# Attention and gated experts on one core: gate weights loaded behind the first exponential, keys turned behind the first scores, loads and stores priced by their own rate

## The chip, the cores and the metric

One core of one Trainium2 chip. The metric is device time of one execution in microseconds.

## What is computed

Eight batches; q, k, v have 8 heads, 576 positions and 64 columns, p has 32 rows a head. Attention runs twice, then each token goes through the expert that its gate picks, or that of the token before it where its local gate is at least 0.5.

```python
p_packed = sm_attn(p, k, v)                # softmax(p k^T / 8) v
out = sm_attn(q, p_packed, p_packed)       # x: 8 x 576 x 512
logits = einsum('bsd,de->bse', x, w_gate)
e = argmax(logits[b, s]) if s == 0 or sigmoid(x @ w_local)[b, s] < 0.5 else prev_e
h = maximum(x[b, s] @ w1[e], 0.0)          # 512 -> 1024
out[b, s] = softmax(logits[b, s])[e] * (h @ w2[e])
```

## The kernel before

The kernel takes one batch after the other. It takes the expert chosen for the batch's first token for the whole batch and mends tokens for which this doesn't hold. Per batch, for two halves of four heads each (Q0 and Q1): the keys are turned (a transpose) into `qn`, scores of p against them go to PSUM (`scores`, L477), an exponential follows (L506), its weights `a` are turned (L515, L520) into `a1T`, the packed values come from L540, are scaled into `zz` (L553) and turned into `ppT` (L561). Against `ppT` the gate of a batch's first token is computed (L701 to L733), which gives the expert `e`; its weights `w1t` and `w2raw` are then fetched by SP. The second attention (L591 to L645) gives `a2t`, cast into `a2h` with a remainder `a2l` (L651, L654). The first layer never forms x: W1 is multiplied with `ppT` (L889 in batch 0, L918 in the others) into `wph` and its remainder `wpl`, and L958 multiplies those with `a2h` and `a2l`; L969 and L973 make `h`; the second layer (L986, L991, L995) multiplies it with `w2s`, a rounded `w2raw` and its remainder (L944, L946). L1009 to L1021 scale by the gate into `o`, which is stored.

In batches 0 and 1 keys and queries are turned on TensorE (`turn_tokens`, L422 and L430, tile `kw` for the long part, `qt` for the rest) and p in `turn_packs` (L458); in the others VectorE turns them (L444, L575). `heat` is a bf16 tile on which dummy matmuls (L217) are run where PE would be idle in the head. `load_small` fetches three small inputs on ScalarE's DMA queue; `wgl` holds `w_gate` in 64 x 8 x 8, in rows of 8 elements, and gets a ninth column from `small` by VectorE (`turn_small`, L296).

All instructions are in an order that is decided when the program is built. Each piece of work is a generator that yields what it needs (`need`: tiles, free slots, a condition, and by whom a tile is consumed). `weave` starts, at each step, a generator that the `Clock` believes ready; `Clock.note` adds each instruction to the modelled time of its engine. DMAs all went to one modelled queue, at `clock.rate` bytes per ns, which keeps the value that was last set. So a price changes which instruction comes first on an engine, and nothing else.

Of the kernel before, what the change touches and what calls it, by code (L numbers as in the profile page):

```python
# [16 lines left out]
DRAM = bass.MemoryType.DRAM  # L17
# [5 lines left out]
NQ = H // HQ  # L23
# [34 lines left out]
class Clock:  # L58
# [69 lines left out]
    def note(self, inst):  # L128
        outs = [x.bass_ap for x in inst.outs if hasattr(x, "bass_ap")]
        ins = [x.bass_ap for x in inst.ins if hasattr(x, "bass_ap")]  # L130
# [6 lines left out]
        dma = inst.opcode == "DMACopy"  # L137
        if dma:
            kind, took = "DMA", min(x.free_size() * x.partition_size() for x in outs + ins if x.space != DRAM) * 4 / self.rate
        else:  # L140
            kind, took = self.price(inst, outs, ins)
        start = max(self.engine(kind), self.engine("SP") if dma else 0.0)
        for x in ins + ([] if dma else outs):
            at, by = self.written.get(self.key(x), (0.0, kind))
# [18 lines left out]
def packed_attn_moe_kernel(  # L163
# [12 lines left out]
    nc = tc.nc  # L176
# [103 lines left out]
    def load_small():  # L280

        clock.rate = 100.0
        nc.scalar.dma_start(out=small[0:2 * H], in_=q[0:2, :, 0, :].rearrange("b h d -> (b h) d"))
        nc.scalar.dma_start(out=small[2 * H:3 * H], in_=w_local.rearrange("(h d) e -> h (d e)", d=D))
        with nc.allow_non_contiguous_dma(reason="rows of 8 elements"):
            nc.scalar.dma_start(out=wgl[:, :, 0:E], in_=w_gate.rearrange("(h d) e -> d h e", d=D))
# [84 lines left out]
    def loads(st):  # L371
# [12 lines left out]
        for name, Q in order:  # L384
# [3 lines left out]
            if name == "q" and isinstance(b, int) and b == 2:  # L388
                yield need(when=lambda: len(sts[1].get("w1", ())) == 2)
            yield need(slot="p_in" if name == "p" else "qn" if blocks else "kv" if name == "v" else ("w2s", "o"))  # L390
            if name == "p":
# [17 lines left out]
    def turn_tokens(st, name):  # L409
# [5 lines left out]
        for Q in range(NQ):  # L415
            yield need(when=lambda: (name, Q) in st and (early or st["second"] or st["valued"] == NQ and (Q == 0 or st["ppT"][Q] is not None)))
            x, rest = st[name, Q]
            for n, hs in enumerate((slice(0, 2), slice(2, 4))):
                yield need(x[:, hs], banks=1, by=("Activation",))
                tp = bank()  # L420
                for c in range(4):
                    nc.tensor.transpose(out=tp[:, 128 * c:128 * c + 128], in_=x[:, hs][:, c // 2, 128 * (c % 2):128 * (c % 2) + 128], identity=ident)  # L422
                yield need(tp, by=("Activation",))
                (nc.vector.tensor_copy if early and Q == 0 and n else nc.scalar.copy)(
                    out=xT[:, Q, hs, 0:256].rearrange("a h (p c) -> a h c p", c=2), in_=tp.rearrange("a (h c p) -> a h c p", h=2, c=2),
                )
                give(tp)
# [24 lines left out]
    def turn_packs(st):  # L452

        yield need(when=lambda: "px" in st)
        yield need(st["px"], slot="pT", banks=1, by=("Activation",))
# [165 lines left out]
    def soften(st, Q, part, m0, m1, sT):  # L621
# [27 lines left out]
        give(sT)  # L649
        yield need(a2t)  # L650
        nc.scalar.copy(out=a2h, in_=a2t)  # L651
# [348 lines left out]
    def store(b, st, i, mask=None):  # L1000
# [23 lines left out]
        if mask is not None:  # L1024
# [4 lines left out]
            )  # L1029
        queue = nc.scalar if isinstance(b, int) and b == B - 1 and i == 3 else nc.sync  # L1030
        queue.dma_start(out=dst, in_=o[:rows])

# [89 lines left out]
    def weave(main):  # L1122
# [3 lines left out]
        while main in threads or any(x.batch < 0 for x in threads):  # L1126
# [7 lines left out]
            while started < B and started <= max(at_batch[0], 0) + AHEAD:  # L1134
# [4 lines left out]
                    slots(st), pack_quarters(st) if early else pack_weights(st, both), splits(st),  # L1139
                    *((turn_small(),) if early else ()), *((early_choice(st),) if started < 2 else ()),  # L1140
                    *((turn_packs(st), turn_tokens(st, "k")) if started < 2 else (turn_keys(st, Q) for Q in both)),
# [148 lines left out]
```

## Time and profile before

| | us |
|---|---|
| median of three runs | 431.81 (431.33 to 433.35) |
| profiled execution | 430.42 |
| its span | 428.6 |
| outside the span | 1.82 |
| PE busy | 410.8 (96%) |
| VectorE busy | 292.4 (68%) |
| ScalarE busy | 180.8 (42%) |
| GpSimd busy | 46.8 (11%) |
| DMA moved | 73.10 MB |

The span is what the hardware profiler recorded from the first to the last instruction. Busy times of different engines overlap. PE is matmul, DVE VectorE, ACT ScalarE, POOL GpSimd, SPq and ACTq the engines' DMA issues. A row of the timeline is a run of like instructions (x16), with its start, how long it took, and in brackets how long the engine had been idle before and what ended that.

### The profile page before, as it was taken

Reading aid. Unit: us, or ns where it says so; the run is one execution under the profiler, and the core shown is the slowest. Engines: PE = TensorE matmul, PEld = TensorE weight load, DVE = VectorE, ACT = ScalarE, POOL = GpSimd, SP = SyncE. Lnnn points to the kernel's source line nnn. Section 1 sums busy time; section 2 is a strip of 40 time slices with the busy share of each in tenths; the row PEclk is TensorE's granted clock in tenths of the full one; section 3 lists DMA queues with packets and bytes.
Section 4 is the critical chain, followed back from the end, with each engine's and each line's share of the span. In section 5 each row is a group of like instructions: output and inputs, shape, how many; then the busy total and the mean of one; then the engine's idle time right before and its main releaser. Section 6 shows DMA issues by size and latency. Waiting matters only on the chain.

```text
span 428.6 us, 9926 instructions
## 1 busy us (share of the span) xinstructions
PE 410.8 (96%) x3784; PEld 320.0 (75%) x3785; DVE 292.4 (68%) x853; ACT 180.8 (42%) x420; POOL 46.8 (11%) x65
## 2 busy tenths in 40 slices
PE   6999999999998999999999999999999999999994
PEld 3646677878885788776888688777887678878883
DVE  1478558887779797749975778749966688547321
ACT  2455453365333633345333544154434533344211
POOL 2001520253130002000110001100030001100000
PEclk9999999999999999999999999999999999999998
DMA  8849739999998599906998299945999430563011
GB/s 222 239 136 326 219 71 160 319 192 211 130 120 297 154 201 151 335 11 211 167 162 308 79 240 133 237 164 158 181 130 269 151 111 0 163 216 125 0 63 57
DMA packets 161671, 73.10 MB, mean 171 GB/s; under 512 B 126288, under 2 KB 141648, under 8 KB 161616
## 3 DMA queue, kind: packets, MB, share of 16 engines
q1 hardware_dynamic: 160624, 72.04, 73.8%
q8 instruction: 32, 0.52, 0.5%
q10 hardware_dynamic: 992, 0.35, 0.3%
q14 instruction: 23, 0.19, 0.1%
HBM read 62.94 MB, written 9.44 MB: 169 GB/s over the span
## 4 chain that ended last, share of the span: by engine, by line
PE 76%; DVE 8%; SPq 5%; DMA 5%; issue 2%; ACT 2%; POOLq 0%; POOL 0%; DVEq 0%; ACTq 0%
PE bank L986 37%; PE bank L958 21%; PE bank L991 4%; PE bank L995 3%; PE bank L540 2%; PE bank L918 2%; DVE wpl L932 2%; PE bank L591 2%; PE bank L515 2%; PE bank L477 2%; DMA kv<-in_q_dram 1%; DMA qn<-in_q_dram 1%; SPq L324 1%; DVE qn L575 1%; DVE h L973 1%
## 5 line engine op out<-in xcount | busy, mean ns | idle before, releaser
L986 PE MATMUL bank<-w2s,h 128*128 128x512 f32 x768 | 207.4, 400 | 4.6 <-DVE w2s L946 3.1
L986 PEld LDWEIGHTS bank<-w2s,h 128*128 128x128 f32 x768 | 135.4, 188 | 35.6 <-issue 5.2
L969 ACT ACTIVATE h<-bank 128x256 fp32r<-128x256 f32 (+1 forms) x128 | 52.9, 413 | 116.8 <-PE bank L958 111.9
L973 DVE SCALAR_TENSOR_TENSOR h<-bank,h 128x256 fp32r<-128x256 f32 x192 | 61.5, 348 | 58.6 <-ACT h L969 58.3
L958 PEld LDWEIGHTS bank<-a2h,wph 128*128 128x128 f32 x256 | 47.0, 188 | 17.4 <-ACT wph L929 2.3
L958 PE MATMUL bank<-a2h,wph 128*128 128x320 f32 (+1 forms) x256 | 56.9, 302 | 0.3
L958 PE MATMUL bank<-a2h,wpl 128*128 128x320 f32 (+1 forms) x256 | 55.9, 298 | 0.1
L958 PE MATMUL bank<-a2l,wph 128*128 128x320 f32 (+1 forms) x256 | 54.6, 294 | 0.0
L654 POOL TENSOR_TENSOR a2l<-a2t,a2h 128x576 fp32r<-128x576 f32 (+2 forms) x17 | 23.4, 1377 | 275.0 <-ACT a2h L651 275.0
L958 PEld LDWEIGHTS bank<-a2h,wpl 128*128 128x128 f32 x256 | 41.0, 188 | 1.0 <-DVE wpl L932 1.0
L958 PEld LDWEIGHTS bank<-a2l,wph 128*128 128x128 f32 x256 | 41.0, 188 | 0.0
L944 ACT CAST w2s<-w2raw 128x512 fp32r<-128x512 f32 x64 | 37.4, 625 | 2.6 <-DMA w2raw<-in_moe_w_dram 2.4
L946 DVE TENSOR_TENSOR w2s<-w2raw,w2s 128x512 fp32r<-128x512 f32 x50 | 32.4, 683 | 0.8 <-ACT w2s L944 0.7
L991 PE MATMUL bank<-w2s,h 128*128 128x512 f32 x64 | 26.0, 406 | 0.0
L995 PE MATMUL bank<-w2s,h 128*64 128x512 f32 x64 | 25.2, 394 | 0.0
L932 DVE TENSOR_TENSOR wpl<-bank,wph 128x512 fp32r<-128x512 f32 x28 | 18.3, 683 | 6.8 <-ACT wph L929 6.8
L946 POOL TENSOR_TENSOR w2s<-w2raw,w2s 128x512 fp32r<-128x512 f32 x14 | 17.9, 1300 | 27.4 <-ACT w2s L944 22.6
L929 ACT CAST wph<-bank 128x512 fp32r<-128x512 f32 x28 | 14.8, 599 | 11.5 <-PE bank L918 11.5
L485 DVE TENSOR_SCALAR_CACHE_REDUCE a<-bank 128x288 f32<-128x288 f32 x32 | 13.3, 454 | 8.7 <-PE bank L477 8.2
L611 DVE STREAM_TRANSPOSE sT<-bank 128x288 f32<-128x288 f32 (+2 forms) x36 | 13.2, 419 | 8.5 <-ACT gate L609 7.9
L651 ACT CAST a2h<-a2t 128x576 fp32r<-128x576 f32 (+2 forms) x18 | 11.1, 625 | 13.2 <-DVE a2t L645 10.3
L575 DVE STREAM_TRANSPOSE qn<-qn 128x1152 f32<-128x1152 f32 x12 | 16.5, 1373 | 0.1
(148 smaller groups left out, 451.4 us busy)
## 6 DMA issues: line engine op xcount, KB each, us to landing
w2raw<-in_moe_w_dram SPq DMA_DIRECT2D x64, 256.0 KB, 7.3
w1t<-in_moe_w_dram SPq DMA_DIRECT2D x14, 1024.0 KB, 5.8
kv<-in_v_dram SPq DMA_DIRECT2D x16, 512.0 KB, 6.3
out_dram<-o SPq DMA_DIRECT2D x31, 256.0 KB, 2.7
qn<-in_k_dram SPq DMA_DIRECT2D x24, 288.0 KB, 7.1
qn<-in_q_dram SPq DMA_DIRECT2D x24, 288.0 KB, 7.5
w1t<-in_moe_w_dram SPq DMA_DIRECT2D x4, 512.0 KB, 6.3
kw<-in_k_dram SPq DMA_DIRECT2D x3, 512.0 KB, 6.8
```

The costliest lines, as they stand in the source:

```text
L575: nc.vector.transpose(out=qT, in_=qT)
L654: eng.tensor_tensor(out=a2l, in0=a2t, in1=a2h.bitcast(F32), op=ALU.subtract)
L929: nc.scalar.copy(out=hi[fh][:, Q], in_=ts[fh, Q])
L932: nc.vector.tensor_tensor(out=lo[fh][:, Q], in0=ts[fh, Q], in1=hi[fh][:, Q].bitcast(F32), op=ALU.subtract)
L944: nc.scalar.copy(out=w[:, 0], in_=raw)
L946: (nc.gpsimd if st["second"] or st["early"] and c > 1 else nc.vector).tensor_tensor(out=w[:, 1], in0=raw, in1=w[:, 0].bitcast(F32), op=ALU ...
L958: nc.tensor.matmul(out=t[:, :GROUP * (m1 - m0)], lhsT=st["wp"][c // 4][wi][:, Q, fs], rhs=a2[ai][Q][:, GROUP * m0:GROUP * m1], start=(n == ...
L969: nc.scalar.activation(out=h[:, :w], in_=t[:, :w], func=AF.Relu)
L973: nc.vector.scalar_tensor_tensor(out=h[:, dst:dst + z - a], in0=t[:, a:z], scalar=0.0, in1=h[:, a:z].bitcast(F32), op0=ALU.max, op1=ALU.su ...
L986: nc.tensor.matmul(out=acc, lhsT=hs[hi], rhs=w[:, wi], start=(c == 0 and n == 0), stop=(c == NC - 1 and n == 2),)
L991: nc.tensor.matmul(out=acc, lhsT=h[:, 256:WIDE + TAIL], rhs=w[:, 0], start=(c == 0), stop=False, skip_group_check=True,)
L995: nc.tensor.matmul(out=acc[0:TAIL], lhsT=h[:, 256:WIDE], rhs=w[:, 1], start=False, stop=(c == NC - 1), skip_group_check=True,)
```

## The change

The load of `wgl` moves from `load_small` into a generator of its own that starts once the exponential of Q0 is issued. The second half of batch 0's keys is turned only after the first half has been scored, and half of its copy goes to VectorE. The packs of batch 1 are turned only after batch 0's expert is chosen. DMAs of ScalarE's queue get a modelled queue of their own, stores a rate of 300 bytes per ns, and the cast of `a2t` says that only ScalarE consumes it. The slot asked for by a q load of the second batch is another one.

```diff
--- before.py
+++ after.py
@@ -136,10 +136,11 @@
             return
         dma = inst.opcode == "DMACopy"
         if dma:
-            kind, took = "DMA", min(x.free_size() * x.partition_size() for x in outs + ins if x.space != DRAM) * 4 / self.rate
+            aside = "Activation" in str(inst.engine)
+            kind, took = "DMA2" if aside else "DMA", min(x.free_size() * x.partition_size() for x in outs + ins if x.space != DRAM) * 4 / self.rate
         else:
             kind, took = self.price(inst, outs, ins)
-        start = max(self.engine(kind), self.engine("SP") if dma else 0.0)
+        start = max(self.engine(kind), self.engine("Activation" if aside else "SP") if dma else 0.0)
         for x in ins + ([] if dma else outs):
             at, by = self.written.get(self.key(x), (0.0, kind))
             start = max(start, at + (LAT if by != kind else 0.0 if kind == "PE" else SAME))
@@ -282,6 +283,11 @@
         clock.rate = 100.0
         nc.scalar.dma_start(out=small[0:2 * H], in_=q[0:2, :, 0, :].rearrange("b h d -> (b h) d"))
         nc.scalar.dma_start(out=small[2 * H:3 * H], in_=w_local.rearrange("(h d) e -> h (d e)", d=D))
+
+    def load_gates():
+
+        yield need(when=lambda: sts[0]["weighed"] > 0)
+        clock.rate = 100.0
         with nc.allow_non_contiguous_dma(reason="rows of 8 elements"):
             nc.scalar.dma_start(out=wgl[:, :, 0:E], in_=w_gate.rearrange("(h d) e -> d h e", d=D))
 
@@ -387,7 +393,7 @@
                 yield need(when=lambda: all("w2" in sts[x] and len(sts[x]["w2"]) == NC for x in (b - 2, b - 1) if "ereg" in sts[x]))
             if name == "q" and isinstance(b, int) and b == 2:
                 yield need(when=lambda: len(sts[1].get("w1", ())) == 2)
-            yield need(slot="p_in" if name == "p" else "qn" if blocks else "kv" if name == "v" else ("w2s", "o"))
+            yield need(slot="p_in" if name == "p" else "qn" if blocks else "kv" if name == "v" else ("kv" if name == "q" and st["second"] else "w2s", "o"))
             if name == "p":
                 if st["pairs"]:
                     st["px"] = load_packs(b, (nc.sync, nc.sync))
@@ -413,7 +419,7 @@
         xT = st[name] = tile_([128, NQ, HQ, HALF], F32, "qn")
         clock.halves[xT.tensor.name] = H * HALF
         for Q in range(NQ):
-            yield need(when=lambda: (name, Q) in st and (early or st["second"] or st["valued"] == NQ and (Q == 0 or st["ppT"][Q] is not None)))
+            yield need(when=lambda: (name, Q) in st and (early and (Q == 0 or st["scored"] > 0) or st["second"] or st["valued"] == NQ and (Q == 0 or st["ppT"][Q] is not None)))
             x, rest = st[name, Q]
             for n, hs in enumerate((slice(0, 2), slice(2, 4))):
                 yield need(x[:, hs], banks=1, by=("Activation",))
@@ -421,7 +427,7 @@
                 for c in range(4):
                     nc.tensor.transpose(out=tp[:, 128 * c:128 * c + 128], in_=x[:, hs][:, c // 2, 128 * (c % 2):128 * (c % 2) + 128], identity=ident)
                 yield need(tp, by=("Activation",))
-                (nc.vector.tensor_copy if early and Q == 0 and n else nc.scalar.copy)(
+                (nc.vector.tensor_copy if early and n else nc.scalar.copy)(
                     out=xT[:, Q, hs, 0:256].rearrange("a h (p c) -> a h c p", c=2), in_=tp.rearrange("a (h c p) -> a h c p", h=2, c=2),
                 )
                 give(tp)
@@ -451,7 +457,7 @@
 
     def turn_packs(st):
 
-        yield need(when=lambda: "px" in st)
+        yield need(when=lambda: "px" in st and (st["early"] or "ereg" in sts[0]))
         yield need(st["px"], slot="pT", banks=1, by=("Activation",))
         tp = bank()
         for g in range(2):
@@ -647,7 +653,7 @@
                 in_=sT[:, r].rearrange("a m n -> a (m n)"),
             )
         give(sT)
-        yield need(a2t)
+        yield need(a2t, by=("Activation",))
         nc.scalar.copy(out=a2h, in_=a2t)
         yield need(a2h)
         eng = nc.vector if part == 0 and Q == 1 else nc.gpsimd
@@ -1028,6 +1034,7 @@
                 out=o[:rows], mask=mask[:rows, i:i + 1].broadcast_to([rows, DM]), data=new[:rows],
             )
         queue = nc.scalar if isinstance(b, int) and b == B - 1 and i == 3 else nc.sync
+        clock.rate = 300.0
         queue.dma_start(out=dst, in_=o[:rows])
 
     def chunks(todo, aside, mask=None):
@@ -1137,7 +1144,7 @@
                 apart = tuple((Q,) for Q in both) if early else (both,)
                 threads.extend(Thread(g, started) for g in (
                     slots(st), pack_quarters(st) if early else pack_weights(st, both), splits(st),
-                    *((turn_small(),) if early else ()), *((early_choice(st),) if started < 2 else ()),
+                    *((load_gates(), turn_small()) if early else ()), *((early_choice(st),) if started < 2 else ()),
                     *((turn_packs(st), turn_tokens(st, "k")) if started < 2 else (turn_keys(st, Q) for Q in both)),
                     *(scores(st, Qs) for Qs in (apart if started != 1 else ((0,), (1,)))), *(keys(st, Qs) for Qs in apart),
                     *((gate_weights(st),) if started < 2 else ()), gates(st),
```

How the order moves, at three places. On PE in the head, before (`kw`, `qt` are keys, `heat` dummies, L477 the scores of Q0 and then Q1):

```order
22 L217 LDWEIGHTS heat
23 L217 MATMUL bank_68<-heat 128x512
24 L422 MATMUL bank_188<-ident,kw 128x128 x4
25 L477 MATMUL bank_193<-qn,pT 32x288 x4
26 L477 MATMUL bank_194<-qn,pT 32x288 x4
27 L422 MATMUL bank_208<-ident,kw 128x128 x4
28 L430 MATMUL bank_214<-ident,qt 128x128
29 L217 LDWEIGHTS heat
...
37 L477 MATMUL bank_225<-qn,pT 32x288 x4
38 L477 MATMUL bank_226<-qn,pT 32x288 x4
```

and now (L428 was L422, L483 was L477, L436 was L430):

```order
24 L218 LDWEIGHTS heat
25 L218 MATMUL bank_68<-heat 128x512
26 L483 MATMUL bank_188<-qn,pT 32x288 x4
27 L483 MATMUL bank_189<-qn,pT 32x288 x4
28 L428 MATMUL bank_202<-ident,kw 128x128 x4
29 L428 MATMUL bank_208<-ident,kw 128x128 x4
30 L436 MATMUL bank_214<-ident,qt 128x128
31 L218 LDWEIGHTS heat
32 L218 MATMUL bank_68<-heat 128x512
...
41 L483 MATMUL bank_227<-qn,pT 32x288 x4
42 L483 MATMUL bank_228<-qn,pT 32x288 x4
```

The scores of Q0 now stand ahead of all three turning steps of Q1, with one dummy more before them.

On VectorE where batch 1's first layer is prepared, before:

```order
164 L973 SCALAR_TENSOR_TENSOR h<-bank_1276,h 128x256
165 L642 TENSOR_TENSOR sT<-sT,sm 128x576
166 L645 STREAM_TRANSPOSE a2t<-sT 128x288 x2
167 L973 SCALAR_TENSOR_TENSOR h<-bank_1298,h 128x256
168 L444 STREAM_TRANSPOSE qn<-qn 128x4x288
169 L760 STREAM_TRANSPOSE lt<-bank_1326 128x160
170 L973 SCALAR_TENSOR_TENSOR h<-bank_1318,h 128x256
171 L407 STREAM_TRANSPOSE p_in<-p_in 128x256
172 L932 TENSOR_TENSOR wpl<-bank_1356,wph 128x512
173 L932 TENSOR_TENSOR wpl<-bank_1357,wph 128x512
```

and now (L651 was L645, L450 was L444, L938 was L932):

```order
164 L979 SCALAR_TENSOR_TENSOR h<-bank_1275,h 128x256
165 L646 RECIPROCAL sm<-sm 128x18
166 L648 TENSOR_TENSOR sT<-sT,sm 128x576
167 L450 STREAM_TRANSPOSE qn<-qn 128x4x288
168 L979 SCALAR_TENSOR_TENSOR h<-bank_1295,h 128x256
169 L938 TENSOR_TENSOR wpl<-bank_1317,wph 128x512
170 L938 TENSOR_TENSOR wpl<-bank_1318,wph 128x512
171 L979 SCALAR_TENSOR_TENSOR h<-bank_1342,h 128x256
172 L651 STREAM_TRANSPOSE a2t<-sT 128x288 x2
173 L938 TENSOR_TENSOR wpl<-bank_1319,wph 128x512
174 L938 TENSOR_TENSOR wpl<-bank_1320,wph 128x512
```

The second pair of `a2t` now stands behind a turn of `qn`, two `h` and two `wpl`.

On VectorE in batch 3, where `w2s` is prepared, before:

```order
382 L932 TENSOR_TENSOR wpl<-bank_2809,wph 128x512
383 L932 TENSOR_TENSOR wpl<-bank_2810,wph 128x512
384 L575 STREAM_TRANSPOSE qn<-qn 128x4x288
385 L973 SCALAR_TENSOR_TENSOR h<-bank_2853,h 128x256
386 L973 SCALAR_TENSOR_TENSOR h<-bank_2853,h 128x64
387 L932 TENSOR_TENSOR wpl<-bank_2811,wph 128x512
388 L1021 TENSOR_SCALAR o<-bank_2537,pe 128x512
389 L932 TENSOR_TENSOR wpl<-bank_2812,wph 128x512
390 L946 TENSOR_TENSOR w2s<-w2raw,w2s 128x512
391 L575 STREAM_TRANSPOSE qn<-qn 128x4x288
```

and now (L952 was L946, L581 was L575):

```order
381 L938 TENSOR_TENSOR wpl<-bank_2752,wph 128x512
382 L938 TENSOR_TENSOR wpl<-bank_2753,wph 128x512
383 L559 TENSOR_SCALAR zz<-bank_2792,rs 128x128 x2
384 L979 SCALAR_TENSOR_TENSOR h<-bank_2779,h 128x256
385 L938 TENSOR_TENSOR wpl<-bank_2754,wph 128x512
386 L938 TENSOR_TENSOR wpl<-bank_2755,wph 128x512
387 L952 TENSOR_TENSOR w2s<-w2raw,w2s 128x512 x2
388 L581 STREAM_TRANSPOSE qn<-qn 128x4x288
```

Two `w2s` now stand ahead of the turn of `qn` that was before all of them.

## Rows read from the trace of the kernel before

**Rows 1.** Windows: length, busy by engine, PEclk, DMA share, GB/s

```profile
0.00:26.00 26.00, 21.37 (x261) 12.81 (x263) 9.74 (x45) 10.41 (x27) 2.71 (x18) 0.93 0.70 194
...
33.20:52.00 18.80, 18.48 (x159) 13.06 (x158) 13.57 (x46) 9.53 (x24) 5.65 (x5) 1.00 0.97 289
...
52.00:104.00 52.00, 51.87 (x590) 40.30 (x592) 38.69 (x130) 25.48 (x63) 12.97 (x15) 1.00 0.85 189
```

**Rows 2.** PE's waits, 52 us to the end: total, times, longest

```profile
PE bank L986 <- DVE w2s L946: 3.1, 3, 1.1
```

**Rows 3.** Timeline, 9 to 14.3: start, us, engine, line

```profile
9.16 0.99 PE L422 MATMUL bank<-ident,kw 128*128 128x128 f32 x4 [2.12 <-DMA kw<-in_k_dram]
...
10.09 1.21 PE L477 MATMUL bank<-qn,pT 64*32 64x288 f32 x16
...
12.35 1.23 PE L217 MATMUL bank<-heat 128*128 128x512 bf16 x4
...
13.03 0.79 ACT L506 ACTIVATE a<-a,nb 128x576 f32<-128x576 f32 x1
...
13.51 0.71 PE L477 MATMUL bank<-qn,pT 64*32 64x288 f32 x16
```

**Rows 4.** Windows of the head, columns as in rows 1

```profile
10.00:11.00 1.00, 1.00 (x17) 0.23 (x16) 0.00 (x0) 0.63 (x1) 0.00 (x0) 0.50 1.14 283
...
13.00:14.00 1.00, 1.00 (x19) 0.26 (x17) 0.00 (x0) 0.92 (x3) 0.00 (x0) 1.00 0.94 301
...
22.00:25.00 3.00, 2.12 (x29) 1.12 (x24) 1.78 (x10) 1.82 (x5) 0.00 (x0) 1.00 0.05 12
```

**Rows 5.** Timeline, 18 to 24.5, VectorE and PE

```profile
18.16 0.15 DVE L296 COPY wgl<-bank 64x8 f32<-64x8 f32 x1
...
19.23 0.35 DVE L553 TENSOR_SCALAR zz<-bank,rs 128x128 f32<-128x128 f32 x1 [0.92 <-PE bank L540]
...
22.30 0.66 PE L422 MATMUL bank<-ident,kw 128*128 128x128 f32 x4
...
22.80 0.25 DVE L720 STREAM_TRANSPOSE et<-es 128x64 f32<-128x64 f32 x1
...
23.84 0.41 PE L458 MATMUL bank<-ident,p_in 128*128 128x128 f32 x2 [0.88 <-DMA p_in<-in_p_dram]
...
24.17 0.31 PE L723 MATMUL bank<-gate,et 128*32 128x32 f32 x4
```

**Rows 6.** DMA queues, 4.5 to 8: packets, MB, share of 16 engines

```profile
q1 hardware_dynamic: 996, 0.91, 87.1%
...
q10 hardware_dynamic: 527, 0.02, 8.3%
```

**Rows 7.** Timeline of ScalarE's DMA issues

```profile
2.45 0.70 ACTq L286 DMA_DIRECT2D wgl<-in_moe_w_gate_dram  x1
```

**Rows 8.** DMA queues, 8 to 12, columns as in rows 6

```profile
q1 hardware_dynamic: 1533, 1.12, 112.7%
```

**Rows 9.** DMA issues, 0 to 40: KB each, median us to landing

```profile
kv<-in_v_dram SPq DMA_DIRECT2D x4, 512.0 KB, 7.8
...
small<-in_q_dram ACTq DMA_DIRECT2D x1, 4.0 KB, 3.0
```

**Rows 10.** Timeline, 81 to 88.5, around batch 1's first layer

```profile
81.02 0.84 DVE L645 STREAM_TRANSPOSE a2t<-sT 128x288 f32<-128x288 f32 x2
...
81.90 0.68 ACT L651 CAST a2h<-a2t 128x576 fp32r<-128x576 f32 x1
...
82.65 1.42 POOL L654 TENSOR_TENSOR a2l<-a2t,a2h 128x576 fp32r<-128x576 f32 x1 [0.36 <-ACT a2h L651]
...
86.83 1.29 DVE L932 TENSOR_TENSOR wpl<-bank,wph 128x512 fp32r<-128x512 f32 x2 [1.48 <-ACT wph L929]
...
88.05 0.45 PE L958 MATMUL bank<-a2l,wph 128*128 128x320 f32 x2
```

**Rows 11.** Timeline of PE near 195

```profile
194.86 1.42 PE L986 MATMUL bank<-w2s,h 128*128 128x512 f32 x5 [1.03 <-DVE w2s L946]
```

## The prediction

> **What bounds the kernel now.** I read the windows first. From 52 us on TensorE is nearly always busy (51.87 of the first 52 us there), and from 33.2 to 52 as well, beside DMA engines at 0.97; only the head is not packed: 21.37 busy of 26.00, and much of that is dummy matmuls on `heat` [rows 1]. PE's waits after 52 us then say what is left there: the largest group is 3.1 us in three places [rows 2]. So an edit late in the kernel can win little, but can lose by making PE wait; whatever shortens the head moves everything behind it, one for one.
>
> In the head I follow the timeline. PE waits 2.12 us for the second half (Q1) of the first keys, although Q0 is turned; it turns part of Q1 at 9.16, only then scores Q0 at 10.09, turns the rest, runs four dummies and scores Q1 at 13.51 [rows 3]. The exponential of Q0 starts at 13.03. The granted clock had fallen to 0.50 after that idle time: sixteen score matmuls took 1.21 us, and 0.71 at 13.51, when it was 1.00 again [rows 3, 4]. The chain goes on through `zz` of Q1 (19.23), `et` (done 23.05), the turn of batch 1's packs L458, which waited 0.88 us for its load, and L723 (24.17), the step that chooses the first expert and so releases the first weights [rows 5].
>
> **The keys.** Scores of Q0 now follow the first turns and one more dummy. Three dummies had ended where the idle time began, 9.16 - 2.12 = 7.04; with 0.3 for the fourth (1.23 for four [rows 3], on a clock partly low, so an upper end) scores run at about 7.35, for 0.71, to 8.05. Q1's keys arrive at 9.16 at the latest. The gate load that leaves this stretch had 8.3% of the DMA engines' time in 3.5 us [rows 6], 0.29 us, so I take 8.87. PE then idles 0.8 us. After an idle of 0.88 us before 23.84 the clock was still 1.00 [rows 4, 5], so I price the turns at full clock: 0.66 per four (L422 at 22.30 [rows 5]), two fours and the last piece some 1.5 us, to about 10.35. ScalarE copies one half and the last piece, VectorE the other half, beside each other; the exponential of Q0 stands behind both ScalarE copies and starts at about 11.0 instead of 13.03. Scores of Q1, behind five dummies, come at about 11.6 instead of 13.51. I take **-2.0** for the chain. The other end: the clock falls again, each four turns cost 0.99 as at 9.16 [rows 3], the last piece some 0.3, five dummies 1.5, and Q1 is scored at 12.8, -0.7.
>
> **The gate load.** It is issued on ScalarE's queue behind the exponential: 11.0 + 0.79 [rows 3], and 0.2 more for the read of its sum, an estimate: 12.0. The issue holds ScalarE 0.70 us [rows 7]; its next step, the copy of Q0's turned weights, is wanted at 13.05, so that is covered; if the exponential slips by over 0.35 us, the copy slips too. How long the load takes amid full DMA queues only the old place shows: issued at 2.45, packets of queue 10 were moved between 4.5 and 8.0, and none from 8 to 12 [rows 6 to 8], so 5.6 us. The ends are 3.0 (the small load) and 7.8 (the values on SP's queue) [rows 9]; I take 5.6, the same transfer: landing 17.6. Who waits: VectorE's small copy into the same tile (L296, now L302; 0.15 us [rows 5]) must follow it, and stands ahead of `zz` of Q1 in VectorE's order. With -2.0 `zz` would run at 17.2; behind the load it runs at 17.75, so of the 2.0 **-1.5** is left. At 3.0 us all 2.0 stay; at 7.8 `zz` runs at 19.95, +0.7. The Trainium skill (DMA: Bandwidth & Descriptors, Queues, rings and completion order) says that a DMA engine takes turns between queues, a packet batch from each; the 527 packets of queue 10 beside 996 of queue 1 in the same stretch [rows 6] agree, and by it the load would again take about 5.6 and the sum stay as it is. The same page (Rules for kernel authors) speaks against the move: issue early, wait late. By that, the load left at the head would cost its 0.3 us of Q1's arrival and spare the wait, and the sum below would be 0.2 us better.
>
> **The packs.** L458 and its wait leave the path to L723. `et` is there at 23.05 and PE free at 22.96 [rows 5], so L723 could run at 23.15 instead of 24.17: **-1.0**. L458 goes behind the choice, among dummies, so it costs nothing as long as its load is there; it landed by 23.84, and its new place in PE's order, six dummies and two score pieces after the choice, comes at 24 or later even 2.5 us earlier; a head 3.5 us shorter would show up to 0.5 of that wait again. Later, the first weights are asked for 2.5 us sooner; the same bytes follow, so the 0.97 stage shifts whole. Head: -1.5 - 1.0 = **-2.5**.
>
> **The planner.** The prices of ScalarE-queue loads and of stores, and whom a copy of `a2t` waits for, take no time; they re-order the later batches. The slot for the second batch's q moves nothing, since q of that batch isn't loaded by that branch. By the order, batch 1 loses: before, `a2t` of Q1 was written from 81.02, cast at 81.90, and its low part was ready at 84.07, four us ahead of the matmul that needs it at 88.05 [rows 10]. Now VectorE does a turn of `qn`, two `h` and two `wpl` first, and the `wpl` wait for packed weights. The packing moved up, ahead of one first-layer group, three second-layer matmuls and the gate's (some 2.4 us of PE, an estimate), so the two `wpl` (1.29) run from 86.83 - 2.4 = 84.4 to 85.7; then the second `h` (some 0.4), to 86.2; `a2t` (0.84) to 87.05, its cast with handovers to 87.9, GpSimd's low part (1.42) to 89.3, and one more handover: the matmul of 88.05 starts at about 89.55, **+1.5**. Nothing (if PE's other work lies before it) and +2.8 (GpSimd now has two `w2s`, 1.29 each, ahead of that low part) are the ends. Batch 3 gains: PE waited 1.03 us for a `w2s` of VectorE at 194.86 [rows 11]; the `wpl` come earlier and the `w2s` ahead of both turns of `qn`. I take **-0.8**, with 0 and -1.03 as ends. The order at the other stalls is the same or moves a piece either way by under a duration of 0.7; 0, with -1 and +1 as ends.
>
> **Sum**: -2.5 + 1.5 - 0.8 = -1.8 us. The profiled execution took 430.42, so 428.6; it lies 1.39 below the median 431.81, against which I forecast **430.0**.
>
> **Rivals.**
> Batch 1 loses nothing: in favour, VectorE stood idle there for 1.48 us before the two `wpl` [rows 10], so they may fit in earlier than I place them; against, the casts that they wait for come behind matmuls whose place PE's order fixes. -2.5 - 0.8 = -3.3, 428.5; with a load of 3.0 us, 428.0.
> The clock falls again: for it, PE still idles in this stretch, and one dummy more is thin cover; against, 0.88 us at 23. Then `zz` moves by 0.6 (the load, issued at 13.0, lands at 18.6): -0.6 - 1.0 + 0.7 = -0.9, 430.9.
> The gate load starves, the slower side: if it is served only as SP's queue drains. That queue's burst is over by 22, when the mean share to 25 is down to 0.05 [rows 4]; landing at 22.0, VectorE stands at its small copy, `zz` of Q1 runs at 22.15, 2.9 late: +2.9 - 1.0 + 0.7 = +2.6, 434.4. It decides from a landing at 19.4, 7.4 us behind the issue, where all gains are gone; SP's 7.8 is just beyond that, the 5.6 of the old place speaks against it.
> The change doesn't do what it says: the exponential stays behind Q1's copies, so if these come as late as before the first scores gain nothing, and the load uses up the packs' 1.0: 431.8.
>
> **Chances.** Forecast 0.42 (own range 429.1 to 431.3), batch 1 free 0.26, clock 0.17, starved load 0.11, nothing moved 0.04. A measurement tells 0.5%, 2.16 us, from no change: faster is below 429.65, slower above 433.97. Faster takes the second case, the lower third of the forecast's and a little of the clock's, 0.41; slower the starved load's, 0.10; same the rest, 0.49. The range leaves out the starved load and the end of the second case: 427.8 to 432.6.
>
> **What would show it.** Right: scores of Q0 at 7.3 at full clock, exponential at 11.0, VectorE waiting for the gate load to 17.6, L723's successor at about 21.7, a wait of 1 to 2 us near 86 before batch 1's first low-part matmul, and none at batch 3. Wrong: a clock of 0.50 at 10 us, a load landing after 19.4, or the late waits of [rows 2] growing by more than the head gives.

## The result and the profile after

The changed kernel took 427.97 us (median of four runs, 426.18 to 429.0), the kernel before 431.88 beside it: a ratio of 0.99 (95% interval 0.9858 to 0.9942), 3.9 us less where 1.8 was forecast. Two later comparisons of the same two kernels (e5 and e12 below) gave 0.9949 (0.9924 to 0.9973; 12 runs against 24) and 0.9937 (0.9913 to 0.9961; 11 against 28), so 2.2 and 2.7 us. One execution of e5 (1381 us, the profiled one, so that e5 has no profile to read) and one of e4 (1009 us) were disturbed and are left out here and below. Faster is settled, at about 0.6%; the first four runs lay at its upper end. The profiled execution took 427.63 with a span of 425.8, 2.8 less than [rows 1]'s kernel.

The windows of the changed kernel, with the columns of [rows 1]:

```profile
0.00:26.00 26.00, 23.53 (x277) 14.29 (x283) 13.62 (x56) 11.47 (x30) 2.71 (x18) 1.00 0.77 217
...
52.00:104.00 52.00, 50.28 (x551) 38.84 (x550) 42.34 (x130) 24.35 (x60) 14.39 (x15) 1.00 0.87 180
```

The head is now packed: 23.53 of 26.00 instead of 21.37. From 52 to 104 there is a new gap, 50.28 instead of 51.87. The timeline of the head, to lay beside [rows 3, 5, 7] (what was L477 is L483 now, L422 L428, L506 L512, L296 L302, L553 L559, L723 L729; L680 is the matmul that uses the gate weights, L720 the exponential of the gate):

```profile
7.65 0.72 PE L483 MATMUL bank<-qn,pT 64*32 64x288 f32 x16
...
8.32 1.08 PE L428 MATMUL bank<-ident,kw 128*128 128x128 f32 x8
...
9.73 0.78 ACT L512 ACTIVATE a<-a,nb 128x576 f32<-128x576 f32 x1
...
11.33 0.71 ACTq L292 DMA_DIRECT2D wgl<-in_moe_w_gate_dram  x1
...
15.19 0.15 DVE L302 COPY wgl<-bank 64x8 f32<-64x8 f32 x1
...
16.27 0.35 DVE L559 TENSOR_SCALAR zz<-bank,rs 128x128 f32<-128x128 f32 x1 [0.92 <-PE bank L546]
...
18.23 0.33 PE L680 MATMUL bank<-wgl,ppT 64*32 64x32 f32 x16 [0.51 <-DMA wgl<-in_moe_w_gate_dram]
...
19.30 0.27 ACT L720 ACTIVATE es<-es 128x64 f32<-128x64 f32 x1
...
20.81 0.31 PE L729 MATMUL bank<-gate,et 128*32 128x32 f32 x4
```

Q1's keys don't keep PE waiting: their turns follow the scores at 8.32 without a bracket. The exponential of Q0 starts at 9.73 (13.03 before), `zz` of Q1 at 16.27 (19.23), the choice of the first expert at 20.81 (24.17), 3.36 earlier. The small copy L302 ran at 15.19, while the load that it was said to wait for came at 18.2 and stopped PE at L680. How long that load took, from the list of DMA issues (KB, us to landing), and the clock at 10 us (0.50 in [rows 4]) and at 135, in windows:

```profile
wgl<-in_moe_w_gate_dram ACTq DMA_DIRECT2D x1, 16.0 KB, 6.9
```

```profile
10.00:11.00 1.00, 0.95 (x18) 0.28 (x17) 0.13 (x1) 0.60 (x2) 0.00 (x0) 1.00 1.17 293
...
135.00:140.00 5.00, 4.45 (x38) 1.42 (x39) 3.52 (x15) 3.63 (x10) 0.00 (x0) 0.66 0.57 206
```

PE's waits from 52 us to the end, beside [rows 2], and the timeline of the new one, beside [rows 10]:

```profile
PE bank L992 <- DVE w2s L952: 2.3, 3, 1.0
...
PE bank L521 <- ACT a L512: 2.0, 1, 2.0
...
PE bank L964 <- POOL a2l L660: 1.6, 1, 1.6
```

```profile
83.07 0.83 DVE L651 STREAM_TRANSPOSE a2t<-sT 128x288 f32<-128x288 f32 x2
...
84.06 0.69 ACT L657 CAST a2h<-a2t 128x576 fp32r<-128x576 f32 x1
...
84.26 1.28 POOL L952 TENSOR_TENSOR w2s<-w2raw,w2s 128x512 fp32r<-128x512 f32 x1 [0.79 <-ACT w2s L950]
...
85.50 1.40 POOL L660 TENSOR_TENSOR a2l<-a2t,a2h 128x576 fp32r<-128x576 f32 x1
...
86.95 0.42 PE L964 MATMUL bank<-a2l,wph 128*128 128x320 f32 x1 [1.59 <-POOL a2l L660]
```

`a2t` of Q1 came late on VectorE, and GpSimd was then still at a `w2s` remainder, so `a2l` began at 85.50, 0.75 after the cast was done, and PE waited 1.59 us: a loss of the size forecast for batch 1. The 1.03 us at 194.86 [rows 11] are gone.

Starts of the first layer in each batch (first L958 or L964 of the timeline) show where the 3.36 went. Batches interleave differently in the two orders, so single differences are good to some tenths:

| | choice | batch 0 | batch 1 | batch 2 | batch 4 | span |
|---|---|---|---|---|---|---|
| before | 24.17 | 33.26 | 87.75 | 139.13 | 239.34 | 428.6 |
| change | 20.81 | 29.92 | 84.43 | 139.84 | 237.10 | 425.8 |
| dummies at 135 (e8) | 20.94 | 29.98 | 84.47 | 138.37 | 237.90 | 426.6 |
| three mended (e11) | 20.24 | 29.80 | 83.57 | 136.50 | 235.74 | 424.5 |

The lead of 3.3 reaches batch 1 whole and is gone at batch 2. The wait took 1.59 of it, and some 1.5 went to the clock, which fell to its lower level (1.2 instead of 2.4 GHz; 0.66 of full in the mean from 135 to 140) behind a wait of 2.02 us at L521. The kernel before has that wait too (2.03 at 136.31, 1.00 granted from 135 to 140).

What such a fall costs in the end is less. The change, and then its third comparison (e12), where the clock stayed up behind the same wait:

```profile
135.55 0.74 PE L521 MATMUL bank<-ident,a 128*128 128x128 f32 x4 [2.02 <-ACT a L512]
...
136.38 3.52 PE L924 MATMUL bank<-w1t,ppT 64*32 64x512 f32 x32
...
151.35 0.45 PE L964 MATMUL bank<-a2h,wph 128*128 128x320 f32 x2
```

```profile
137.07 0.74 PE L521 MATMUL bank<-ident,a 128*128 128x128 f32 x4 [2.02 <-ACT a L512]
...
137.85 1.95 PE L924 MATMUL bank<-w1t,ppT 64*32 64x512 f32 x32
...
151.97 0.46 PE L964 MATMUL bank<-a2h,wph 128*128 128x320 f32 x2
```

L924 takes 1.57 longer at the lower clock, but L964 at 151 comes only 0.9 later behind the wait's end (15.80 instead of 14.90), for the stretch from batch 2's first layer to there is 0.58 shorter (from 139.84; from 139.88 in e12). The other profiles, but for the re-ordered e7, fall into the same two groups: 15.8 where the clock fell there (e1, e2, e3, e10), 14.9 where it didn't (e4, e8, e9, e11). So 0.9 is the price of this fall.

### The profile page after: what moved, and what is told of

Its sections match the earlier page's. It is cut to its first block, busy times and chain, and to the rows that moved or that the text cites. A ratio compares the mean times of both kernels' runs of the same rounds, so it can differ in the third digit from the quotient of the medians.

```text
span 425.8 us, 9932 instructions
## 1 busy us (share of the span) xinstructions
PE 410.0 (96%) x3778; PEld 319.5 (75%) x3784; DVE 295.2 (69%) x854; ACT 180.0 (42%) x419; POOL 47.0 (11%) x65
## 4 chain that ended last, share of the span: by engine, by line
PE 76%; DMA 6%; DVE 6%; SPq 5%; issue 2%; ACT 2%; POOL 1%; POOLq 0%; DVEq 0%; ACTq 0%
PE bank L992 36%; PE bank L964 21%; PE bank L997 3%; PE bank L924 3%; PE bank L1001 3%; PE bank L546 2%; DMA w1t<-in_moe_w_dram 2%; PE bank L597 2%; PE bank L521 2%; PE bank L483 2%; DMA wgl<-in_moe_w_gate_dram 2%; DMA v_rest<-in_v_dram 2%; DMA qn<-in_q_dram 1%; SPq L346 1%; DVE h L979 1%
## 5 line engine op out<-in xcount | busy, mean ns | idle before, releaser
L964 PEld LDWEIGHTS bank<-a2h,wph 128*128 128x128 f32 x256 | 46.9, 188 | 17.6 <-issue 2.6
L964 PE MATMUL bank<-a2h,wph 128*128 128x320 f32 (+1 forms) x256 | 56.8, 302 | 0.1
L964 PE MATMUL bank<-a2l,wph 128*128 128x320 f32 (+1 forms) x256 | 54.9, 295 | 1.6 <-POOL a2l L660 1.6
L964 PE MATMUL bank<-a2h,wpl 128*128 128x320 f32 (+1 forms) x256 | 55.3, 297 | 0.0
L964 PEld LDWEIGHTS bank<-a2l,wph 128*128 128x128 f32 x256 | 41.1, 188 | 1.9 <-POOL a2l L660 1.9
L964 PEld LDWEIGHTS bank<-a2h,wpl 128*128 128x128 f32 x256 | 40.9, 188 | 0.4 <-DVE wpl L938 0.4
L952 DVE TENSOR_TENSOR w2s<-w2raw,w2s 128x512 fp32r<-128x512 f32 x50 | 32.3, 677 | 2.1 <-ACT w2s L950 2.1
L938 DVE TENSOR_TENSOR wpl<-bank,wph 128x512 fp32r<-128x512 f32 x28 | 18.0, 679 | 4.8 <-ACT wph L935 4.8
L952 POOL TENSOR_TENSOR w2s<-w2raw,w2s 128x512 fp32r<-128x512 f32 x14 | 18.2, 1313 | 24.4 <-ACT w2s L950 24.2
L935 ACT CAST wph<-bank 128x512 fp32r<-128x512 f32 x28 | 14.9, 596 | 10.9 <-PE bank L924 10.9
L581 DVE STREAM_TRANSPOSE qn<-qn 128x1152 f32<-128x1152 f32 x12 | 16.4, 1370 | 0.3 <-DMA qn<-in_q_dram 0.3
L450 DVE STREAM_TRANSPOSE qn<-qn 128x1152 f32<-128x1152 f32 x12 | 16.4, 1367 | 0.0
L512 ACT ACTIVATE a<-a,nb 128x576 f32<-128x576 f32 x16 | 12.4, 776 | 9.3 <-DVE nb L500 9.3
```

The lines of the kernel that those rows point to most:

```text
L450: nc.vector.transpose(out=kT, in_=kT)
L581: nc.vector.transpose(out=qT, in_=qT)
L938: nc.vector.tensor_tensor(out=lo[fh][:, Q], in0=ts[fh, Q], in1=hi[fh][:, Q].bitcast(F32), op=ALU.subtract)
L952: (nc.gpsimd if st["second"] or st["early"] and c > 1 else nc.vector).tensor_tensor(out=w[:, 1], in0=raw, in1=w[:, 0].bitcast(F32), op=ALU ...
L964: nc.tensor.matmul(out=t[:, :GROUP * (m1 - m0)], lhsT=st["wp"][c // 4][wi][:, Q, fs], rhs=a2[ai][Q][:, GROUP * m0:GROUP * m1], start=(n == ...
```

## The experiments

Two theories at the start. A: the head gained because Q1's keys no longer held it, and what holds it next is a load (gate weights, packs, first weights); behind it the gain is given back at single waits. B: the new order alone made it, and loads don't matter; or, later, waits behind the head are hidden anyway. Every run but the last has one edit, or in e2 the two edits of the keys together; e5 and e12 have none. The diffs show only the changed part of a line.

**e1, the load back at the head.**

```diff
-        yield need(when=lambda: sts[0]["weighed"] > 0)
-        clock.rate = 100.0
...
-    (load_gates(), turn_small())
+    (turn_small(),)
```

> The changed kernel with the gate load alone put back among the first loads; the order of every engine but for that one DMA is that of the change. Theory A (the load held up Q1's keys and the earlier keys gave part of the gain): Q1's keys are turned 0.5 to 0.9 us later than 8.32, PE idles before that, the exponential of Q0 comes at 10.3 to 11 instead of 9.73; but PE no longer waits 0.51 us for the gate load, so the choice of the first expert (20.81 in the change) comes at about 20.7 to 21.4, and the time is within 0.7 us of the change. If the granted clock falls again after that idle time, the choice comes at 22 or later and 1 to 1.5 us are lost. Theory B (the order alone made the gain, the load costs the keys nothing): keys at 8.3, no wait for the load, choice at 20.1, 0.7 us faster than the change.

Measured: 428.7 against 430.88, ratio 0.995 (0.9923 to 0.9977). Its timeline of PE and one window:

```profile
6.34 1.11 PE L428 MATMUL bank<-ident,kw 128*128 128x128 f32 x4 [0.32 <-DMA kw<-in_k_dram]
...
7.46 1.91 PE L218 MATMUL bank<-heat 128*128 128x512 bf16 x4
...
9.31 1.21 PE L483 MATMUL bank<-qn,pT 64*32 64x288 f32 x16
...
22.26 0.31 PE L729 MATMUL bank<-gate,et 128*32 128x32 f32 x4
```

```profile
8.00:9.00 1.00, 1.00 (x4) 0.19 (x2) 0.19 (x1) 0.00 (x0) 0.00 (x0) 1.00 1.18 297
```

The choice came 1.45 late, at 22.26 as A had it for a low clock. PE was still at its slow pace of the start: four dummies took 1.91 (1.03 in the change, at 6.70), scores 1.21. The 1.00 of the window doesn't speak against it: the trace has no entry on the clock before its first rise, which comes at 10.5 us here and between 4.7 and 7.5 in all other profiles, and a stretch without an entry is printed as 1.00. Q1's keys are turned 2.13 later than in the change (10.45), and these dummies and scores make up 1.37 of it. The other 0.76 lies ahead of the dummies (7.46 instead of 6.70), where PE waited 0.32 us for keys of Q0. That the load caused either isn't shown: the kernel before has it at the same place without such a wait, and e4, without it, waits longer for Q0's keys. There was no wait for the gate load. The time is not apart from the change's, so e1 decides nothing between A and B.

**e2, the old order of the keys.**

```diff
-(early and (Q == 0 or st["scored"] > 0) or st["second"]
+(early or st["second"]
...
-if early and n else nc.scalar.copy
+if early and Q == 0 and n else nc.scalar.copy
```

> The changed kernel with the old order of the keys: first quarter of Q1 turned ahead of the scores of Q0, both Q1 copies on ScalarE; nothing behind the head moves. Theory A (keys that land early gave most of it, and without the 2.12 us of idle time the clock stays up): keys at 8.3, exponential of Q0 only 0.6 to 1.3 us later than 9.73, since it stands behind one more copy; choice of the expert 0.6 to 1.3 later than 20.81. Theory B (the order of the scores gave most of it): the exponential at 12 or later, the choice 2 to 3 us later, time back near that of before.

Measured: 428.73, ratio 0.9953 (0.9929 to 0.9978). Timeline:

```profile
8.59 0.66 PE L428 MATMUL bank<-ident,kw 128*128 128x128 f32 x4 [1.10 <-DMA kw<-in_k_dram]
...
11.18 0.78 ACT L512 ACTIVATE a<-a,nb 128x576 f32<-128x576 f32 x1
...
17.18 0.35 DVE L559 TENSOR_SCALAR zz<-bank,rs 128x128 f32<-128x128 f32 x1 [0.92 <-PE bank L546]
...
18.45 0.31 PE L680 MATMUL bank<-wgl,ppT 64*32 64x32 f32 x16
...
21.05 0.31 PE L729 MATMUL bank<-gate,et 128*32 128x32 f32 x4
```

The exponential is 1.45 late and `zz` of Q1 0.91, yet the choice only 0.24: the load was there in time, so what the change wins with its key order it mostly waits for at L680. B (exponential at 12 or later, choice 2 to 3 later) falls; A had the kind right and both sizes wrong (0.6 to 1.3 expected for each).

**e3, the load 4 us earlier.**

```diff
-sts[0]["weighed"] > 0
+sts[0]["scored"] > 0
```

> The changed kernel with the gate load issued ahead of Q1's copies on ScalarE, once Q0's scores are issued, some 3 to 4 us earlier; PE's, VectorE's, GpSimd's and SP's order stays word for word. Theory A (the late load costs the change 0.5 to 0.7 us on the way to the choice): it lands at about 14 to 15, PE doesn't wait for it, the choice comes at about 20.1 to 20.3 and the time is 0.5 to 0.7 us better. Theory B (the load delays whatever is in flight, wherever it stands): the keys or the values come later and the choice stays at 20.8 or later.

Measured: 428.01, ratio 0.9935 (0.9914 to 0.9957). Timeline:

```profile
16.62 0.35 DVE L559 TENSOR_SCALAR zz<-bank,rs 128x128 f32<-128x128 f32 x1 [0.92 <-PE bank L546]
...
17.89 0.31 PE L680 MATMUL bank<-wgl,ppT 64*32 64x32 f32 x16
...
20.48 0.31 PE L729 MATMUL bank<-gate,et 128*32 128x32 f32 x4
...
24.01 0.41 PE L464 MATMUL bank<-ident,p_in 128*128 128x128 f32 x2 [0.69 <-DMA p_in<-in_p_dram]
```

The load is issued at 7.10 and PE doesn't wait for it; from `zz` of Q1 (16.62) to the choice it is 3.86 instead of 4.54, so the late load costs 0.68. But then PE waits 0.69 at the packs, and the first weights are used at 26.84, where they were at 26.74: the next load takes it back. The time is not apart from the change's.

**e4, batch 1's remainder on VectorE.**

```diff
-eng = nc.vector if part == 0 and Q == 1 else nc.gpsimd
+eng = nc.vector if (part == 0 or st["second"]) and Q == 1 else nc.gpsimd
```

> The changed kernel with the remainder a2l of Q1 in batch 1 on VectorE instead of GpSimd, where it stood behind two remainders of w2s; PE's, ScalarE's and SP's order stays. Theory A (the 1.59 us that PE waits near 87 us is GpSimd's queue, and goes through to the end): the remainder is ready at about 85.9 instead of 86.9, the wait shrinks to about 0.5, and the time is 0.9 to 1.1 us better. Theory B (later batches give it back, since VectorE now carries 0.75 us more in a busy stretch): the wait shrinks and the end moves by under 0.3 us.

Measured: 427.13, ratio 0.9923 (0.9896 to 0.995). The wait (PE's waits from 52 us) goes from 1.59 to 0.84, where 0.5 was expected: so about half of it came from GpSimd, by its queue and by 1.40 us for the remainder where VectorE takes 1.16; the other half stays, with `a2t` as late on VectorE. From the first rise to the last stage the clock did not fall. The wait, and a row of the head:

```profile
PE bank L964 <- DVE a2l L660: 0.8, 1, 0.8
```

```profile
7.62 0.33 PE L436 MATMUL bank<-ident,qt 128*128 128x128 f32 x1 [1.53 <-DMA qt<-in_k_dram]
```

Its choice was 0.72 later than the change's in this profile (21.53), for Q0's last key piece held PE for 1.53 us; its span was still the shorter, 425.2. Of these 1.3 us, 0.9 is the fall of the clock that it lacked. Whether the end moved by 0.9 for the edit the intervals can't say.

**e5 and e12, the change again**, unedited.

> The change itself once more, beside the others. Theory A (the spread of single runs comes from whether the clock falls after the waits of 1.6 us near 87 and 2.0 us near 135): the choice of the first expert comes at 20.8 within 1 us, both waits are there again, and the granted clock falls behind none, one or both of them, at about 1.7 us each; median 426.5 to 428.5. Theory B (the first profile was a lucky head): choice at 22 or later, median over 429.

> The change itself beside the three others, since its profile of the second time was disturbed. Theory A: choice of the first expert at 20.8 within 1 us, waits of 1.6 us near 87 and 2.0 near 135, 0.4 to 0.9% faster than before. Theory B (a lucky first head): choice at 22 or later, under 0.4% faster.

Measured: 428.98 and 428.12, the ratios above; e5 lies between what A (up to 428.5) and B (over 429) expected. In e12 the choice came at 21.35. The windows show where the clock fell in it:

```profile
85.00:90.00 5.00, 3.42 (x13) 2.58 (x13) 4.91 (x11) 1.45 (x3) 4.92 (x6) 0.81 1.19 164
...
135.00:140.00 5.00, 2.90 (x45) 1.20 (x38) 4.14 (x22) 3.02 (x8) 0.00 (x0) 1.00 0.87 316
```

It fell behind the wait of 1.6 us and not behind the one of 2.0; in the first profile it was the other way round, in e1 and e2 it fell behind both, in e9 behind neither, though both waits are there. Single runs of the change spread by 4.9 us (426.2 to 431.0 in 27), and time and the run's mean granted clock go against each other (correlation -0.61; 0.999 in the fastest, 0.988 in the slowest): falls are a part of the spread, not all of it.

**e6, the kernel before with seven dummies in its gap** (they are kept out of the planner's sums).

```diff
+keep_warm(7 if early and Q == 1 and n == 0 else 0)
```

> The kernel before with seven more dummies in PE's gap of 2.12 us behind Q0's turns; all other orders word for word. Theory A (the fallen clock made up 0.7 to 1 us of the old head): no fall at 9 to 12 us, scores of Q0 0.72 instead of 1.21, exponential of Q0 at about 12.2 instead of 13.03, choice 0.6 to 1.0 earlier than 24.17 unless the packs' load at 23.8 holds it. Theory B (the chain, or the packs' load, hides the clock): the choice stays within 0.3 us of 24.17, time unchanged.

Measured: 431.3 against 431.35, ratio 1.0003 (0.998 to 1.0026). Timeline and windows:

```profile
10.24 0.71 PE L477 MATMUL bank<-qn,pT 64*32 64x288 f32 x16
...
12.24 0.79 ACT L506 ACTIVATE a<-a,nb 128x576 f32<-128x576 f32 x1
...
23.70 0.41 PE L458 MATMUL bank<-ident,p_in 128*128 128x128 f32 x2 [1.72 <-DMA p_in<-in_p_dram]
...
24.03 0.31 PE L723 MATMUL bank<-gate,et 128*32 128x32 f32 x4
```

```profile
10.00:11.00 1.00, 1.00 (x20) 0.37 (x19) 0.00 (x0) 0.64 (x1) 0.00 (x0) 1.00 1.13 310
...
25.00:30.00 5.00, 5.00 (x36) 2.42 (x35) 3.63 (x12) 1.56 (x4) 0.00 (x0) 0.71 0.49 165
```

The scores are at full speed, the exponential 0.79 earlier, and the choice where it was: the packs' load holds it, as B said. So the low clock at 10 us [rows 4] cost the old kernel nothing up to the choice. Here it fell later instead, behind the longer wait, and the first layer began later than before (34.69 instead of 33.26), so the equal time alone would not show that.

**e7, the packs in their old place.**

```diff
-"px" in st and (st["early"] or "ereg" in sts[0])
+"px" in st
```

> The changed kernel with the packs of batch 1 turned ahead of the choice again; the head's order is the change's up to there, later batches are re-ordered by the planner. Theory A (the packs' load lands at 23.5 to 24.2 whatever the chain does, since SP's queue sets it): PE waits at the packs for 2 to 3 us, the choice comes at 23.8 to 24.6, and the head's gain of 3.4 us is nearly all gone: the edits of keys and load are worth nothing without this one. Theory B (terms add, as the prediction had them): the choice comes about 1.0 later than 20.8, at 21.8.

Measured: 436.09, ratio 1.0129 (1.0097 to 1.0162). Timeline:

```profile
23.12 0.66 PE L464 MATMUL bank<-ident,p_in 128*128 128x128 f32 x2 [2.56 <-DMA p_in<-in_p_dram]
...
23.71 0.42 PE L729 MATMUL bank<-gate,et 128*32 128x32 f32 x4
```

PE waits 2.56 us, although the exponential of Q0 starts at 9.67 as in the change; the choice is 2.90 later, and of the head's 3.36 us 0.46 are left. The rest of the loss comes after the head, where the later batches are re-ordered (4.2 us of waiting at L521 instead of 2.0, and 0.50 granted from 140 to 145); it was not taken apart. A holds in the head: the keys and the load are worth almost nothing there without this edit.

**e8, seven dummies in the wait at 135** (out of the planner's sums, into the bank that the transposes then fill).

```diff
+[nc.tensor.matmul(out=tps[0], lhsT=heat[:, :128], rhs=heat, start=True, stop=True)
+    for _ in range(7 if isinstance(st["b"], int) and st["b"] == 3 and Q == 0 else 0)]
```

> The changed kernel with seven dummies in PE's wait of 2.0 us near 135, between the scores and the turned weights of batch 3; all other orders word for word. Theory A (the clock falls behind that wait in some runs, 1.7 us each time): no fall there, granted clock 1.00 at 130 to 145, median 0.5 to 1.7 us better than the change's and a smaller spread. Theory B (the fall is not due to the idle time): it falls as often, median unchanged or 0.2 slower.

Measured: 428.72, ratio 0.9933 (0.9907 to 0.9958). The window, and the timeline at batch 4:

```profile
135.00:140.00 5.00, 4.44 (x45) 2.17 (x45) 4.17 (x16) 4.16 (x11) 0.00 (x0) 1.00 0.59 211
```

```profile
234.03 1.09 PE L924 MATMUL bank<-w1t,ppT 64*32 64x512 f32 x16 [1.43 <-DMA w1t<-in_moe_w_dram]
```

No fall, and batch 2 starts 1.47 earlier than in the change, of which 0.9 is left at 151 us. Then PE stood 1.43 us at L924 for weights that SP asked for at 224.32 (223.13 in the change), behind its narrow q and k loads and three stores; the gain was gone. So the median stayed, as B had it, but not for B's reason. That the dummies kept the clock up is likely and not shown: with them it fell in neither of two profiles (e8, e11), without them behind this wait in five of eight.

**e9, the load priced on the one modelled queue; e10, stores at the old rate.**

```diff
-aside = "Activation" in str(inst.engine)
+aside = False
```

```diff
-        clock.rate = 300.0
```

> The changed kernel with the planner's queue of its own for ScalarE's loads taken back; nothing else edited. The planner now believes that the gate load lands behind all of SP's loads and pads PE's order with eleven dummies ahead of the turn of Q0's zz and puts more work ahead of the choice. Theory A (the price is what lets the moved load pay): the zz of Q1 comes about 2 us later than 16.27, the choice at 23 to 24.5 instead of 20.8, the time is 2 to 3.5 us worse than the change, near that of before. Theory B (dummies fill time in which PE waits anyway): choice within 0.7 us of 20.8, same time.

> The changed kernel with stores priced by the old rate; the order is the change's up to batch 2, and at batch 3 a turn of qn stands ahead of the first w2s again, as before. Theory A (my step on batch 3): PE waits about 1.0 us for that w2s near 193 again, and the end is 0.6 to 1.0 us later. Theory B (later loads of weights set the pace behind it): the wait is there, and the end moves by under 0.4 us.

Measured: e9 433.68, ratio 1.0056 (1.0037 to 1.0075), slower than before and 5.6 slower than the change beside it (A expected 2 to 3.5); e10 429.92, ratio 0.9971 (0.9949 to 0.9994). Rows of e9's timeline, then the one of e10's:

```profile
18.85 0.35 DVE L559 TENSOR_SCALAR zz<-bank,rs 128x128 f32<-128x128 f32 x1 [2.43 <-PE bank L546]
...
24.80 0.31 PE L729 MATMUL bank<-gate,et 128*32 128x32 f32 x4
```

```profile
195.08 1.43 PE L992 MATMUL bank<-w2s,h 128*128 128x512 f32 x5 [1.02 <-DVE w2s L952]
```

e9: the planner, believing in a late load, filled the head with dummies; `zz` of Q1 2.58 later, the choice 4.0. e10: the wait of batch 3 is back, and the end of the profile 2.6 later than the change's, with a fall of the clock at 135 in both. 1.0 of it is the wait; the rest comes at other places of the re-ordered batches and was not taken apart. The median is 1.8 us above the change's beside it, more than A's 0.6 to 1.0, so the price of stores is worth more than the one wait.

**e11, three mended**: e3, e4 and e8 together.

> The changed kernel with the load earlier, the remainder of batch 1 on VectorE and the dummies at 135, together. Theory A (each wait goes through to the end): choice at 20.1 to 20.5, wait at 87 us of 0.5 to 0.9 instead of 1.6, no fall of the clock at 135, 1.5 to 3 us better than the change. Theory B (the weights of batch 4 and the first weights set the pace: PE gets there earlier and waits for their loads): waits of 1 us or more for w1t near 40 and 234, 0 to 1 us better.

Measured: 426.09 against 431.04, ratio 0.9868 (0.984 to 0.9897), and 428.12 for the change beside it: the best of the kernels. Its waits from 52 us:

```profile
PE bank L924 <- DMA w1t<-in_moe_w_dram: 1.1, 1, 1.1
```

No fall of the clock to the last stage, a choice at 20.24, waits of 0.8 at L964 and 0.4 at L521, and about 2.0 us better than the change, as A had it; of B there is the wait for batch 4's weights, 1.1.

## Why the prediction was wrong

The direction held; the size did not. Of the 3.9 us, 1.2 to 1.7 did not come back in the two later comparisons (2.2 and 2.7 us): so much is the luck of the first four runs, and the forecast of 1.8 is short of what remains by 0.4 to 0.9. That 427.97 lies in the range is luck too, for its low end came from the rival in which batch 1 loses nothing (428.5), and batch 1 did lose. The step that failed is the head, -2.5 by forecast and -3.36 in the profile (20.81; the choice comes at 20.69 to 21.53 in e4, e8, e10 and e12, whose heads have the same edits, so -2.6 to -3.5), and in it the term of the keys: the exponential came 1.27 us before its forecast, 0.55 of it because Q1's keys came earlier than I took, 0.72 because their turns and copies took less.

- **Keys, -2.0; measured -2.96** at `zz` of Q1 (-1.6 to -2.9 in e4, e8, e10 and e12, so the first profile had one of the good heads). I let Q1's keys arrive at 8.87 and priced an idle PE; they were there at 8.32, and PE had no wait. The turns took 1.08 instead of 1.3, the copies ran beside each other, and the exponential came at 9.73 instead of 11.0, although scores of Q0 ran at 7.65 and not at 7.35. That the clock would stay up was right. Single edits split the 2.96, one profile each: the old head with its clock kept up has `zz` at 18.25 (e6, -0.98); the old order with the load out of the way at 17.18 (e2, -1.07; keys turned at 8.59 instead of 9.66); the new order 16.27 (-0.91). So the keys came 0.6 to 1.1 us earlier without the load at the head (8.59 against 9.16 before and 9.66 in e6), where I took 0.29 from its share of the DMA engines' time; single profiles scatter by some tenths and more (e4).
- **Gate load, +0.5; measured +0.68, at another place.** The step "VectorE's small copy must follow it" was wrong: that copy fills another column and ran 3 us ahead of the landing. The load held PE at L680, and then the gate's exponential (L720, 19.30) behind two copies on ScalarE; with the load early the way from `zz` to the choice is 0.68 shorter (e3). It took 6.9 us, not 5.6, but did not starve: it landed at 18.2, so the rival on the slower side is refuted. The Trainium skill (DMA: Bandwidth & Descriptors, Queues, rings and completion order) says that the DMA engines take turns between queues; 498 packets of the gate load's queue beside 1264 of SP's from 14.0 to 18.3 us agree. The same page's rule to issue early (Rules for kernel authors) is borne out from 11.33 back to 7.10 (e3); at the very head the load has a price that the rule doesn't name, keys turned at 9.16 and 9.66 (before and e6) instead of 8.59 (e2).
- **Packs, -1.0: right in size beside the others, wrong in kind.** From `zz` of Q1 to the choice it is 4.94 before and 3.86 in e3, so -1.08. But I added it as a term of its own. The packs' load holds PE until 23.1 to 24.0, whatever the chain does (e3, e6, e7), and is a floor for the old choice: under it the clock was worth nothing (e6) and keys and load together 0.46 (e7), and with the chain at 20.8 the edit is worth 2.9.
- **Batch 1, +1.5; measured 1.59**, in part by luck: I had VectorE's late `a2t` alone in the sum and GpSimd's `w2s` only as an end of the range; by e4 about half of the wait is GpSimd's. **Batch 3, -0.8; measured -1.03**, by the mechanism named (e10).
- **Other batches, 0; measured -1.0** in shorter waits, and +0.9 in this profile for a fall of the clock that no term had. I asked after the clock in the head alone.

Head -3.4, waits after 52 us -0.4 (6.5 to 6.1 in all, by the lists of PE's waits: +1.6, -1.0 and -1.0), clock +0.9 make -2.9; the span shows -2.8. This is one pair of profiles, and good to some tenths.

## What to carry to other kernels

Where several loads and a chain meet at one step, its time is the latest of them, and what single edits win there can't be added: find each one's landing, and cost an edit by what is latest without it. A wait on a busy TensorE can cost more than itself, since the clock may fall behind it (0.9 us more here); where the wait can't be removed, dummies in it are worth a try, but look for the load that limits next. A build-time planner's price is part of an edit: moving a load without pricing it right made the kernel slower than before (e9). And a head read from one profile can be off by the spread of its loads: repeat the profile before a term is called wrong.

## What was not expected of the hardware

The same wait (1.59 us near 87, 2.02 near 135) was followed by a lower granted clock in some executions and not in others of the same order; a fall behind the second cost 0.9 us, though its matmuls took 1.57 longer. At the start PE reached full speed at 10.5 us in one profile (e1) and at 4.7 to 7.5 in the others, with the same dummies from 1.64 on; why is open, for e4 waited longer on its keys and was at full speed behind it (four dummies in 1.03). And 16 KB of gate weights in rows of 32 bytes took 6.9 us to land, where 64 KB of packs issued at 18.66 took 4.5, and 2.0 with nothing beside them at 0.78 (landings of `p_in` in the change).
